# Two shifted patterns summed by accumulating transfers, and a further fill behind a run, in a one-core attention and MLP kernel

## The chip, the cores and the metric

The kernel runs on one core of a Trainium2 chip. The metric is the device time in microseconds of one execution. Three runs of the kernel before gave a median of 676.95 us (676.89 to 676.99).

## The reference

```python
def _A_ref(x, wq, wk, wv, wo):
    q = (x @ wq).reshape(B, S, H, Dh).transpose(0, 2, 1, 3)
    k = x @ wk
    v = x @ wv
    scores = jnp.einsum("bhqd,bkd->bhqk", q, k) * (Dh ** -0.5)
    p = softmax(scores, axis=-1)
    o = jnp.einsum("bhqk,bkd->bhqd", p, v)
    return o.transpose(0, 2, 1, 3).reshape(B, S, H * Dh) @ wo

def _B_ref(x, w1, w2):
    return silu(x @ w1) @ w2

xn = layernorm(x)
s = _A_ref(xn, wq, wk, wv, wo)
g = silu(_B_ref(xn, w1, w2))
return x + s * g
```

B = 1, S = 2048, D = 512, H = 32 heads of Dh = 16 that share one key and one value head, and an MLP width of F = 1792. Everything is bfloat16.

## The kernel before

The scores are worked out transposed: one block is 128 keys by 512 queries of one head. Queries come in four chunks of 512 and heads in eight groups of four, so there are 32 groups (chunk and four heads), each with 16 key tiles of four blocks: 2048 blocks. TensorE computes the four heads of a key tile in four row strips of its array (K is 16, padded to 32), and the products with the values in four column strips, in which a 17th column of ones gives the softmax's denominator. The results of a group accumulate in one PSUM bank, `psO`.

Two engines take the exponentials. ScalarE takes two blocks at a time out of `psA0` or `psA1` into one of eleven `pa_sb` buffers (`exp_A`, L576). VectorE takes one block at a time out of the banks `psD`, its second half `D1`, or `psF` (`exp_D`, L614): it adds a constant, clips at zero and rounds to int16, and these 16 bits read as bfloat16 are a rough exponential. The error is evened out by three such patterns of the same block, shifted by 0, 43 and 85 in the integer, with weights that are folded into three copies of the values (`vaug_sb`, filled by `evac_V`). GpSimd makes the two shifted patterns of a whole key tile with one 64-bit integer addition each (`shift`, L639). So a block of ScalarE's needs one product with the values (`emit_PV`, L698), and a block of VectorE's needs three. VectorE's patterns lie in four places (three in `ph_sb`, one in parts of `x_sb` once these are free), each with a buffer for each of the three patterns; `free_slot` picks a place and `may_D` says whether a place's old patterns have all been read.

The MLP and the projections are "jobs" (`emit_job`, L338): matmuls in column strips into `psF`, then a tanh on ScalarE (L1014) and a two-tensor operation on VectorE that makes a silu of it (L1046). A group's end is normalised by VectorE in four steps: `gn1` transposes `psO` (L769), `gn2` takes the reciprocal (L777), `gn3` multiplies (L786, two inputs in SBUF), `gn4` transposes back (L796). `final_add` (L1025) adds x, also with two inputs in SBUF, and stores the result from SyncE.

No engine orders itself: the class `Sched` keeps a model of each engine's time (`Sched.model`), and one Python loop at build time writes out all engines' instruction lists by it, with semaphore waits where one engine's work depends on another's. At each step the loop fills TensorE's column time in "slots" (four matmuls side by side) with jobs or products, and then issues a score run (`score_run`): the two blocks of ScalarE's next exponential, and, through `fill_D`, up to two blocks for VectorE into those banks that are free at that time. A new VectorE tile is taken from the end of its group's list of key tiles, ScalarE's from the beginning; a group's last three tiles are left to ScalarE (`LEAD = 3`) while VectorE begins the next group. `advance_v` settles the order on VectorE between evictions and the other tasks that `v_cand` offers. `held` tells whether a buffer has products left to be read; `filler` issues matmuls with zeros where TensorE would fall idle too long.

At the start ("front") x is loaded, the first four 128-row tiles are normalised (statistics by `stats`, L354, and `aggr`, L357, on VectorE, the root on ScalarE by `rstd_sqrt`, L368), and the rest follows beside the first groups.

Of the kernel before, what the change touches and what calls it, by code (L numbers as in the profile page):

```python
# [22 lines left out]
PH_SHIFT = (0, 43, 85)  # L23
PH_W = (0.2265625, 0.1787109375, 0.1416015625)
PH_ONE = 127 * 128
PH_BIAS = 65
NPH = len(PH_SHIFT)
LN2 = 0.6931471805599453
# [7 lines left out]
class Sched:  # L36
# [5 lines left out]
    def __init__(self):  # L42
        self.queues = {}
        self.done = {}
        self.clock = {}
        self.snap = {}
        self.last_w = {}
        self.readers = {}
        self.flagged = {}
        self.lanes = {}  # L50
        self.at = {}
        self.free = dict(pe=1.2, a=1.7, v=0.85, gp=0.7, sp=0.7)
        self.act_end = 0.0
        self.act_ends = []
        self.pe_mode, self.pe_last, self.pe_len, self.pe_tiles = None, 1.0, 0.0, set()
        self.pe_runs = []

# [37 lines left out]
    def model(self, eng, lane, cost, r):  # L95
        if lane:
            t = max(self.free[eng], r) + 0.05
            self.free[eng] = t
            return t + (cost or 3.0)
        if eng == "pe":  # L100
            mode, tiles, cols = cost or ("full", [None] * 4, 128)
            t = r
            for tile in tiles:
                if mode != self.pe_mode:
                    t = max(t, self.pe_last + self.pe_len + self.SWITCH)
                    self.pe_tiles = set()
# [17 lines left out]
        self.free[eng] = t + (cost or 0.4)  # L124
        return self.free[eng] + self.SEM
# [71 lines left out]
def bass_recurrent_scan__grouped_kv_mqa__dense_activation_silu__prompt_kernel(  # L197
# [39 lines left out]
    NPAIR, LEAD_PAIR = 1, 1  # L237
    NF, F_FROM, F_LEFT, F_LATE, DENSE_END, HOLD, F_BEHIND = 14, 0.05, 9, 3, 0.97, 10, 0

    with ExitStack() as es:  # L240
# [18 lines left out]
        ph_sb = [sb(f"ph{j}_sb", [P, NPS, 4 * NQ], I16) for j in range(NPH)]  # L259
# [13 lines left out]
        eps_sb = sb("eps_sb", [P, 1], FP32)  # L273
        mhalf_sb = sb("mhalf_sb", [P, 4], FP32)
# [80 lines left out]

        def aggr(t):
            op("v", lambda e: e.bn_aggr(mv_sb[:, t, :], stats_sb[:, t, :]), reads=[("st", t)], writes=[("mv", t)], cost=0.155)  # L357

        def rstd_pow(c):
            sl = slice(4 * c, 4 * c + 4)  # L360
            op("gp", lambda e: e.tensor_scalar(rstd_sb[:, sl], mv_sb[:, sl, 1], LN_EPS, None, op0=ALU.add),
               reads=[("mv", t) for t in tiles(c)], writes=[("rstd", c)])
            op("gp", lambda e: e.tensor_tensor(rstd_sb[:, sl], rstd_sb[:, sl], mhalf_sb[:, :], ALU.pow),  # L363
               reads=[("rstd", c), "mhalf"], writes=[("rstd", c)])
# [111 lines left out]
        for t in tiles(0):  # L476
            stats(t)
        for t in tiles(0):
            aggr(t)
# [121 lines left out]
        def ph_ap(j, sl, a, b):  # L601
            if sl < 3:
                return ph_sb[j][:, sl, a:b]
            return x_sb[:, 4 * j:4 * j + 4, :].rearrange("p a b -> p (a b)").bitcast(I16)[:, a:b]

        def ph_key(j, sl, p):
            return ("ph", j, sl, p) if sl < 3 else ("x", 4 * j + p)

        def exp_D(blks):
# [8 lines left out]
            for b in blks:  # L618
                p = b["pos"]
                owe(tile[0], b["i"], tile[1], 1, ph_ap(0, sl, 512 * p, 512 * p + 512).bitcast(BF16), ph_key(0, sl, p), K.at[d])  # L620
# [8 lines left out]
        shifts = []  # L629

        def shift(tile, idx):
            sl, n = slot_of[idx], len(rows_of[idx])
            for j in range(1, NPH):
                if n < 4:
                    d = op("v", lambda e, j=j: e.tensor_scalar(ph_ap(j, sl, 0, NQ * n), ph_ap(0, sl, 0, NQ * n), float(PH_SHIFT[j]), None,
                                                               op0=ALU.add),
                           reads=[ph_key(0, sl, p) for p in range(n)], writes=[ph_key(j, sl, p) for p in range(n)], cost=0.4)
                else:
                    d = op("gp", lambda e, j=j: e.int64_add(ph_ap(j, sl, 0, 4 * NQ).bitcast(I64), ph_ap(0, sl, 0, 4 * NQ).bitcast(I64),  # L639
                                                            PH_SHIFT[j] * 0x0001000100010001),  # L640
                           reads=[ph_key(0, sl, p) for p in range(4)], writes=[ph_key(j, sl, p) for p in range(4)], cost=1.03)
                for p, i in rows_of[idx].items():
                    owe(tile[0], i, tile[1], 1 + j, ph_ap(j, sl, 512 * p, 512 * p + 512).bitcast(BF16), ph_key(j, sl, p), K.at[d])

        def may_D(blks):
            sl = slot_of[blks[0]["idx"]]
            return not any(held(ph_key(j, sl, p)) for j in range(1, NPH) for p in range(4)) and \
                not any(held(ph_key(0, sl, b["pos"])) for b in blks)
# [8 lines left out]
        def emit_PV(t, cap):  # L657
# [7 lines left out]
            while n < cap:  # L665
                cand = sorted((p for p in pend[gi] if p["at"] <= t + 0.216 * n and vready(p["kt"] // 4, t)), key=lambda p: p["at"])
# [48 lines left out]
        def plan_D(gi, rows):  # L715
            owed[gi] += len(rows) * (NPH - 1)
            for i in rows:
                planned[gi][i] += NPH - 1
# [47 lines left out]
        def gn1(tk):  # L766
# [4 lines left out]
            task("gn2", gn2, 0.25, gi=gi, reads=[("otr", sl)], writes=[("rcp", sl)])  # L771
# [9 lines left out]
        def gn3(tk):  # L781
# [5 lines left out]
               reads=tk["reads"], writes=tk["writes"], cost=tk["cost"])  # L787
# [235 lines left out]
        def final_add(eng, tt, src, dst_key, queue="sp"):  # L1023
            slot = tt % NOB
            op(eng, lambda e: e.tensor_tensor(ob_sb[:, slot, :], src, x_sb[:, 12 + tt % 4, :], ALU.add),  # L1025
               reads=[dst_key, ("x", 12 + tt % 4)], writes=[("ob", slot)], cost=0.42)
# [52 lines left out]
        def free_slot(gi):  # L1079

            used = {slot_of[o["idx"]] for o in dst["open"] + dst["fifo"]}
            best = None
            for sl in range(NPD):
                if sl in used or (sl == 3 and not all(("nm", n) in tok for n in range(12))):
                    continue
                keys = {ph_key(j, sl, p) for j in range(NPH) for p in range(4)}
# [49 lines left out]
        def v_cand():  # L1136

            tv = K.free["v"] - 0.084
            cand = [(max(tv, K.ready("v", tk["reads"], tk["writes"])), tk) for tk in tasks if all(n in tok for n in tk["need"])]
            d, blks = 1e9, dst["fifo"][:1]  # L1140
            if blks and may_D(blks):
# [3 lines left out]
                if len(two) == 2 and (two[0]["bank"], two[1]["bank"]) == ("D", "D1") and two[0]["idx"] == two[1]["idx"] and may_D(two):  # L1145
                    d2 = max(tv, K.ready("v", ["D", "D1"], [ph_key(0, slot_of[b["idx"]], b["pos"]) for b in two]))
                    if d2 <= d + 0.1 and meets(d + 0.735) >= meets(d2 + 1.27):
# [29 lines left out]
        def target(t):  # L1177
# [9 lines left out]
            x = max(f, idle - 0.43)  # L1187
            return min(max(rel, x), need) if x <= need + SLIP else need

        def score_run(t):  # L1190
            t = max(t, release())
            if ast["tile"] is None and not left[group_A()]:
# [4 lines left out]
                if tanh_ready(K.act_end - 0.33):  # L1197
# [17 lines left out]
            if tanh_ready(K.act_end - 0.33):  # L1215
# [5 lines left out]
        def fill_D(t, free):  # L1221

            banks = sorted(free_banks(t + SLIP), key=lambda b: (b == "F", K.ready("pe", [], [b])))
            keep = 0
            if "F" in banks and jobs and behind(F_BEHIND) and next_job(t):
# [3 lines left out]
            for bank in banks[:max(0, len(banks) - keep)]:  # L1229
# [3 lines left out]
                if not pick and len(dst["open"]) < 2:  # L1233
# [30 lines left out]
        while state["g"] < NGRP or front or jobs or jst["open"] or tasks:  # L1264
            t = max(now, min(K.pe_next("col"), K.pe_next("full")))
            if t > 2000.0:
                raise ValueError(f"the order does not end {state} {jobs[:3]} {jst} {tasks} {dst} {ast}")
            advance_v(t + 0.05)
            more = group_A() < NGRP
            if tanh_ready(K.act_end - 0.33 if more else t):  # L1270
# [10 lines left out]
            if more:  # L1281
                last, aim = needed(), target(t)
                slots = min(4, int((last - t - K.SWITCH) / 0.2163), max(0, int((aim - t - K.SWITCH) / 0.2163 + ROUND)))
# [5 lines left out]
            if slots > 0:  # L1289
# [11 lines left out]
                if dense_first:  # L1301
# [9 lines left out]
                if can and not dense_first and slots > did:  # L1311
                    did += emit_job(t, slots - did)
            if more and not blocked:
# [3 lines left out]
                score_run(t)  # L1317
                now = 0.0
# [35 lines left out]
        def store(k, queue):  # L1354
            op(queue, lambda e: e.dma_start(ov[:, t0 + k, :], ob_sb[:, k, :]), reads=[("ob", k)], writes=[("out", t0 + k)], lane=f"st{k}{queue}")

# [64 lines left out]
```

## Time and profile before

| | before |
|---|---|
| median of the runs | 676.95 us (676.89 to 676.99) |
| profiled execution: time, span | 676.97 us, 675.0 us |
| busy TensorE, VectorE, ScalarE, GpSimd | 651.4, 588.9, 663.9, 369.1 us |
| exponentials on ScalarE (two blocks each) | 676 |
| evictions on VectorE (one block each) | 696 |
| shifts on GpSimd (INT64_ADD) | 348 |
| tanh on ScalarE | 72 |
| VectorE's waits for its score blocks in psD | 57.0 us |
| first exponential starts, last one ends | 10.49 us, 667.83 us |

The span runs from the first to the last instruction of the profiled execution; the rest of its time lies around it. "Busy" is the union of an engine's instructions. In the groups, a row has the line, engine and operation, what it writes and reads, the shapes and the count, then busy time and mean duration, then the engine's idle time before these instructions and what ended it. In the waits, a row has who waited for whom, the sum in us, the number of waits and the longest.

### The profile page before, as it was taken

What the parts mean: (1) busy time and instruction counts of PE and PEld (TensorE: products, weight loads), DVE (VectorE), ACT (ScalarE), POOL (GpSimd) and SP (SyncE); (2) the same over time, 40 slices, a digit from 0 to 9 for tenths busy, and PEclk for the clock granted to TensorE, in tenths of its full rate; (3) what the DMA queues carried; (4) which work ended last, traced back from release to release, by engine and by line L of the source; (5) the groups of instructions that cost most, each with busy time, mean ns of one, the idle gap of its engine ahead of it and who ended that gap; (6) DMA issues with size and microseconds to landing.
All of it is one profiled execution on the core that took longest, in us unless ns stands there. A gap on an engine that the chain in (4) does not pass through costs nothing.

```text
span 675.0 us, 18633 instructions
## 1 busy us (share of the span) xinstructions
PE 651.4 (96%) x8167; PEld 184.3 (27%) x8174; DVE 588.9 (87%) x1005; ACT 663.9 (98%) x762; POOL 369.1 (55%) x373
## 2 busy tenths in 40 slices
PE   8999999999999999999999999999999999999997
PEld 4422222222222222222222222222222222222221
DVE  7898788888798979999898988899898988888996
ACT  6999999999999999999999999999999999999997
POOL 3155455564555646565564655566564646654653
PEclk9999999999999999999999999999999999999999
DMA  6340000000000001000000000010000000000110
GB/s 178 134 146 2 1 2 1 2 2 1 2 1 2 2 17 34 18 1 2 2 1 2 1 2 2 1 33 18 17 2 2 2 2 1 2 2 1 34 33 32
DMA packets 12337, 12.50 MB, mean 19 GB/s; under 512 B 2528, under 2 KB 11744, under 8 KB 12256
## 3 DMA queue, kind: packets, MB, share of 16 engines
q1 hardware_dynamic: 11680, 10.78, 5.2%
q8 instruction: 64, 1.05, 0.7%
q10 hardware_dynamic: 576, 0.52, 0.2%
q14 instruction: 17, 0.14, 0.1%
HBM read 8.95 MB, written 2.10 MB: 16 GB/s over the span
## 4 chain that ended last, share of the span: by engine, by line
ACT 78%; PE 14%; DVE 3%; issue 1%; POOL 1%; DMA 1%; SPq 0%; POOLq 0%
ACT pa_sb L576 73%; PE psA L546 5%; ACT t_sb L1014 5%; PE psO L698 4%; PE psF L338 4%; DVE ph_sb L614 1%; DMA x_sb<-in_A_x_dram 1%; DVE stats_sb L354 1%; POOL ph_sb L639 1%; POOL rstd_sb L363 0%; DVE xn_sb L375 0%; PE psD L546 0%; PE psD L386 0%; PE psD L417 0%; DVE kTa_sb L429 0%
## 5 line engine op out<-in xcount | busy, mean ns | idle before, releaser
L576 ACT ACTIVATE pa_sb<-psA 128x1024 bf16<-128x1024 f32 x676 | 642.9, 1198 | 1.9 <-PE psA L546 1.7
L639 POOL INT64_ADD ph_sb<-ph_sb x290 | 300.7, 1049 | 221.8 <-DVE ph_sb L614 221.8
L614 DVE TENSOR_SCALAR ph_sb<-psD 128x512 int16<-128x512 f32 x527 | 351.8, 682 | 54.7 <-PE psD L546 47.9
L698 PE MATMUL psO<-ph_sb,vaug_sb 128*32 128x512 bf16 x1740 | 215.6, 383 | 0.2
L698 PE MATMUL psO<-pa_sb,vaug_sb 128*32 128x512 bf16 x1360 | 206.2, 383 | 0.4 <-ACT pa_sb L576 0.4
L546 PE MATMUL psA<-qT_sb,kTa_sb 32*128 32x512 bf16 x692 | 134.2, 385 | 6.8 <-ACT pa_sb L576 5.0
L546 PE MATMUL psA<-qT_sb,kTb_sb 32*128 32x512 bf16 x652 | 126.4, 384 | 7.9 <-ACT pa_sb L576 7.0
L546 PE MATMUL psD<-qT_sb,kTb_sb 32*128 32x512 bf16 x330 | 118.4, 384 | 0.4 <-DVE ph_sb L614 0.4
L546 PE MATMUL psD<-qT_sb,kTa_sb 32*128 32x512 bf16 x307 | 111.7, 384 | 0.1
L639 POOL INT64_ADD x_sb<-x_sb x58 | 60.2, 1050 | 49.7 <-DVE x_sb L614 49.7
L614 DVE TENSOR_SCALAR x_sb<-psD 128x512 int16<-128x512 f32 x110 | 74.2, 680 | 10.5 <-PE psD L546 9.1
L546 PEld LDWEIGHTS psA<-qT_sb,kTa_sb 32*128 32x128 bf16 x692 | 32.4, 91 | 148.2 <-ACT pa_sb L576 136.0
L338 PE MATMUL psF<-xnT_sb,w_sb 128*32 128x512 bf16 x896 | 70.4, 384 | 0.0
L546 PEld LDWEIGHTS psA<-qT_sb,kTb_sb 32*128 32x128 bf16 x652 | 30.6, 91 | 144.1 <-ACT pa_sb L576 136.6
L338 PE MATMUL psF<-w_sb,u_sb 128*32 128x512 bf16 x896 | 69.0, 384 | 0.0
L698 PEld LDWEIGHTS psO<-ph_sb,vaug_sb 128*32 128x32 bf16 x1740 | 53.4, 95 | 50.4 <-issue 33.8
L698 PEld LDWEIGHTS psO<-pa_sb,vaug_sb 128*32 128x32 bf16 x1360 | 50.6, 94 | 44.1 <-issue 33.2
L698 PE MATMUL psO<-x_sb,vaug_sb 128*32 128x512 bf16 x348 | 60.9, 384 | 0.0
L1014 ACT ACTIVATE t_sb<-psF 128x512 bf16<-128x512 f32 x72 | 56.6, 786 | 0.0
L1046 DVE SCALAR_TENSOR_TENSOR u_sb<-t_sb,psF 128x512 bf16<-128x512 bf16 x56 | 38.3, 683 | 6.1 <-ACT t_sb L1014 5.0
L614 DVE TENSOR_SCALAR ph_sb<-psF 128x512 int16<-128x512 f32 x53 | 35.9, 678 | 0.0
L546 PEld LDWEIGHTS psD<-qT_sb,kTb_sb 32*128 32x128 bf16 x330 | 28.2, 91 | 0.8 <-issue 0.7
(124 smaller groups left out, 351.6 us busy)
## 6 DMA issues: line engine op xcount, KB each, us to landing
w_sb<-in_B_w_dram SPq DMA_DIRECT2D x2, 1792.0 KB, 8.7
x_sb<-in_A_x_dram SPq DMA_DIRECT2D x18, 128.0 KB, 2.2
out_dram<-ob_sb SPq DMA_DIRECT2D x14, 128.0 KB, 1.7
x_sb<-in_A_x_dram SPq DMA_DIRECT2D x3, 512.0 KB, 7.1
wop_sb<-in_A_wo_dram SPq DMA_DIRECT2D x1, 512.0 KB, 5.6
wq_sb<-in_A_wq_dram SPq DMA_DIRECT2D x1, 384.0 KB, 6.7
x_sb<-in_A_x_dram ACTq DMA_DIRECT2D x2, 128.0 KB, 2.9
kTb_sb<-kTa_sb SPq DMA_DIRECT2D x16, 16.0 KB, 1.8
```

What stands on the lines that cost most here:

```text
L338: r = e.matmul(bank[32 * i:32 * i + 32, :], lhsT=lhsT[:, 32 * i:32 * i + 32], rhs=rhs, start=start, stop=stop, tile_position=(0, 32 * i), ...
L354: op("v", lambda e: e.bn_stats(stats_sb[:, t, :], x_sb[:, t, :]), reads=[("x", t)], writes=[("st", t)], cost=0.687)
L546: return e.matmul(ap, lhsT=kT_sb[g % 2][32 * i:32 * i + 32, kt * P:(kt + 1) * P], rhs=qT_sb[32 * i:32 * i + 32, c % 2, g // 2, :], start=T ...
L576: d = op("a", lambda e: e.activation(pa_sb[:, sl, :], psA[k][:, :], ACT.Exp, scale=ESCALE), reads=["A%d" % k], writes=[("pa", sl)], cost=2 ...
L614: d = op("v", lambda e: e.tensor_scalar(ph_ap(0, sl, 512 * pos, 512 * pos + m), src, float(PH_ONE + PH_BIAS), 0.0, op0=ALU.add, op1=ALU.ma ...
L639: d = op("gp", lambda e, j=j: e.int64_add(ph_ap(j, sl, 0, 4 * NQ).bitcast(I64), ph_ap(0, sl, 0, 4 * NQ).bitcast(I64), PH_SHIFT[j] * 0x0001 ...
L698: r = e.matmul(psO[32 * i:32 * i + 32, cs], lhsT=vaug_sb[:, p["v"], p["kt"], :], rhs=p["ap"], start=s0, stop=s1, tile_position=(0, 32 * i) ...
L1014: op("a", lambda e: e.activation(t_sb[:, n % 2, :], bank_ap(b), ACT.Tanh, scale=0.5 if jb[0] == "h" else 0.25), reads=[b], writes=[("t", n ...
L1046: op("v", lambda e: e.scalar_tensor_tensor(out=dst, in0=t_sb[:, n % 2, :], scalar=1.0, in1=src, op0=ALU.add, op1=ALU.mult), reads=tk["read ...
```

## The change

**Two patterns summed.** The shifts become 0, 42 and 88, and the first two patterns get the same weight (0.1953125). For a whole key tile that is started late enough before its group's end (at least `SUML` = 5 of the group's tiles left, or a tile of the next group; 9 in the last group; not in the front), GpSimd makes the pattern shifted by 42 and then issues a transfer within SBUF that adds the unshifted pattern to it in bfloat16. The sum needs one product with the values in place of two. The third pattern is then made in place over the unshifted one (`flush_later`), once the transfer has landed or, in a tile that isn't summed, once its products have been read. The model books 0.9 us of GpSimd for the issue and 4.7 us from issue to landing, and 2.8 us between two landings.

**Places of pairs.** A place now has two buffers instead of three, and there are six places instead of four (nine buffers in `ph_sb`, three in `x_sb`).

**Two-tensor operations put off.** The model now has VectorE's operations with two inputs in SBUF (`gn3`, `final_add`) wait for a GpSimd operation that is under way, and `v_cand` puts such a task off by up to 8 us (`PATIENCE`) while that wait would be over 0.2 us (`DEFER`), except in the last two groups.

**A further fill behind a run.** After a score run `extra_fill` gives one more block to a bank of VectorE's that is free or becomes free within 0.3 us (`XWAIT`), if by the model VectorE starts its next block more than 0.25 us (`XGAIN`) plus the waiting time sooner than with the next run's fill, and fewer than seven (`XHOLD`) of ScalarE's `pa_sb` buffers have products left.

**Smaller parts.** In the front, ScalarE makes the mean and the variance of the second tile by two activations with a sum (`stats_act`), and VectorE those of the other three. There are 13 warm-up matmuls instead of 15, and the jobs are spread from the 16th tile on instead of the 12th. ScalarE's two stores at the end become one. A fill by `row_want`, a longer run (`TWIN`) and other choices are in the code but switched off by the values in `RULES`, which hold for the whole run (`PLAN` is "A" alone); the limit `KEEP` for fillers goes from 0.65 to 0.6.

```diff
-PH_SHIFT = (0, 43, 85)
-PH_W = (0.2265625, 0.1787109375, 0.1416015625)
+PH_SHIFT = (0, 42, 88)
+PH_W = (0.1953125, 0.1953125, 0.1416015625)
...
+SUM_LAND = 4.7
...
     def model(self, eng, lane, cost, r):
+        if lane and eng == "gp":
+            t = max(self.free[eng], r + 0.25)
+            self.gp_runs.append((t, t + 0.9, True))
+            self.free[eng] = t + 0.92
+            self.sums = max(self.sums + 2.8, t + SUM_LAND)
+            return self.sums
...
-    NPD = 4
-    NPS = 3
+    SUML_END, DEFER, PATIENCE = 9, 0.2, 8
+    NPD = 6
+    NPB = 9
-    NWARM = 15
+    NWARM = 13
-    NFRONT = 12
+    NFRONT = 16
...
+        A=(0.2, 3.0, 0.6, 10, 1.2, 2.0, 0, 12, 0.2, 3, 3, 0.0, 0.25, 0.43, 0, 0.33, 0, 0, 5, 9, 0.3, 7),
...
-        ph_sb = [sb(f"ph{j}_sb", [P, NPS, 4 * NQ], I16) for j in range(NPH)]
+        ph_sb = sb("ph_sb", [P, NPB, 4 * NQ], I16)
...
+        def stats_act(t):
+            r = D ** -0.5
+            op("a", lambda e: e.activation(scr_sb[:, 1:2], eps_sb[:, 0:1], ACT.Sqrt), ...)
+            op("a", lambda e: e.activation(t_sb[:, 0, :], x_sb[:, t, :], ACT.Copy, scale=1.0 / D, accum_out=mv_sb[:, t, 0:1]), ...)
+            op("a", lambda e: e.activation(nm_sb[:, 0:1], mv_sb[:, t, 0:1], ACT.Copy, scale=r), ...)
+            op("a", lambda e: e.activation(t_sb[:, 1, :], x_sb[:, t, :], ACT.Square, scale=-r, bias=nm_sb[:, 0:1],
+                                           accum_out=mv_sb[:, t, 1:2]), ...)
...
         def shift(tile, idx):
...
+            flush_later(K.ready("gp", first, other_))
+            d = op("gp", lambda e: e.int64_add(whole(1, sl), whole(0, sl), PH_SHIFT[1] * 0x0001000100010001),
+                   reads=first, writes=other_, cost=1.03)
+            if idx in summed:
+                d = op("gp", lambda e: e.dma_start(whole(1, sl, dt=BF16), whole(0, sl, dt=BF16), accum_op=ALU.add),
+                       reads=first, writes=other_, lane=f"sum{sl}")
+            owe_D(tile, idx, 1, 2, K.at[d])
...
+            later.append(dict(tile=tile, idx=idx, sl=sl, at=K.at[d] if idx in summed else None))
...
+        def flush_later(t):
+            for x in list(later):
...
+                if x["at"] > t + 0.1 if x["at"] is not None else any(held(k) for k in first):
+                    continue
+                later.remove(x)
...
+                    d = op("gp", lambda e, sl=sl: e.int64_add(whole(0, sl), whole(0, sl), PH_SHIFT[2] * 0x0001000100010001),
+                           reads=first, writes=first, cost=1.03)
+                owe_D(x["tile"], x["idx"], 0, 3, K.at[d])
...
+                    if DEFER < 9 and tk["kind"] in ("gn3", "add") and state["g"] < NGRP - 2:
+                        end = K.lock(x + 0.13)
+                        if end > x + DEFER and x < tk.setdefault("due", x + PATIENCE):
+                            x = end - 0.13
...
+        def extra_fill():
+            t = K.pe_last + K.pe_len
+            if sum(held(("pa", k)) for k in range(NPA)) >= XHOLD or group_A() >= NGRP or ...:
+                return
+            advance_v(t + 0.05)
+            vfree = K.free["v"] + 0.62 * len(dst["fifo"]) + ...
+            ride = max(needed(), t + 0.2) + 0.43
...
+                    r = max(t, K.ready("pe", [], [b]))
+                    gain = max(vfree, ride) - max(vfree, r + 0.43)
+                    if r <= t + XWAIT and gain > XGAIN + XCOST * (r - t):
...
+            fill_D(best[0], [0, 1, 2, 3], [best[1]])
...
-                        plan_D(new[0], rows)
                         dst["idx"] += 1
+                        if not front and len(rows) == 4 and (new[0] > group_A() or len(left[new[0]]) >= (SUML_END if new[0] == NGRP - 1 else SUML)):
+                            summed.add(dst["idx"])
+                        plan_D(new[0], rows, NPH - (dst["idx"] in summed))
...
         warm(NWARM, psF[:, :], "F")
-        for t in tiles(0):
+        stats_act(1)
+        for t in (0, 2, 3):
             stats(t)
...
-        store(0, "a")
         copy(1, ob_sb[:, 1, :], ("ob", 1), bank_ap("D1"), "D1")
-        store(1, "a")
+        op("a", lambda e: e.dma_start(ov[:, t0:t0 + 2, :], ob_sb[:, 0:2, :]), ...)
```

More of the change, by code (lines that the diff above doesn't have):

```diff
@@ L56, in __init__ @@
         self.pe_runs = []
+        self.gp_runs, self.tt_runs = [], []
+        self.sums = 0.0
+        self.next_gp = 1e9
     def deps(self, eng, reads, writes):
@@ L627, in exp_D, with whole, spare @@
                     shifts.append((tile, idx))
-        shifts = []
+        shifts, summed, later = [], set(), []
+        def whole(j, sl, n=4, dt=I64):
+            return ph_ap(j, sl, 0, n * NQ).bitcast(dt)
+        def spare(sl):
+            busy = {slot_of[o["idx"]] for o in dst["open"] + dst["fifo"]} | {x["sl"] for x in later} | {slot_of[a[1]] for a in shifts} | {sl}
+            for m in range(NPD):
+                if m not in busy and not any(held(ph_key(j, m, p)) for j in range(2) for p in range(4)):
+                    if 2 * m + 1 < NPB or all(("nm", n) in tok for n in range(12)):
+                        return m
+            return None
@@ new lines, in shift @@
+            if sl2 is not None:
+                d = op("gp", lambda e: e.int64_add(whole(0, sl2), whole(0, sl), PH_SHIFT[2] * 0x0001000100010001),
+                       reads=first, writes=[ph_key(0, sl2, p) for p in range(4)], cost=1.03)
+                owe_D(tile, idx, 0, 3, K.at[d], sl2)
+                return
+            later.append(dict(tile=tile, idx=idx, sl=sl, at=K.at[d] if idx in summed else None))
+            K.next_gp = min([x["at"] for x in later if x["at"] is not None], default=1e9)
```

202 lines of the change are left out of this document (157 added, 45 removed).

## The prediction

> **What bounds the kernel now.** I read the page first. ScalarE is busy for nearly the whole span, TensorE and VectorE a little less, and the clock is full in every slice.
>
> ```profile
> PE 651.4 (96%) x8167; PEld 184.3 (27%) x8174; DVE 588.9 (87%) x1005; ACT 663.9 (98%) x762; POOL 369.1 (55%) x373
> ```
>
> The chain of waits shows what ScalarE's time is made of.
>
> ```profile
> 226.34 3.67 ACT pa_sb L576 x4
> 230.00 0.49 ACT t_sb L1014
> 230.50 11.00 ACT pa_sb L576 x12
> ```
>
> Exponentials of two score blocks follow each other every 11.00/12 = 0.917 us, and a tanh adds 0.49 us. 675 x 0.917 + 72 x 0.49 = 654 us; with the first exponential's start (10.5), its own 1.2, 7.2 after the last and about 2 of stalls, that is the span of 675.0. The profiled execution took 676.97 (1.97 outside the span) and the median of the runs is 676.95, so I work from the median. Nothing but fewer exponentials, a shorter front or a shorter tail can shorten this kernel. The groups show who takes the other blocks.
>
> ```profile
> L576 ACT ACTIVATE pa_sb<-psA 128x1024 bf16<-128x1024 f32 x676 | 642.9, 1198 | 1.9 <-PE psA L546 1.7
> L639 POOL INT64_ADD ph_sb<-ph_sb x290 | 300.7, 1049 | 221.8 <-DVE ph_sb L614 221.8
> L614 DVE TENSOR_SCALAR ph_sb<-psD 128x512 int16<-128x512 f32 x527 | 351.8, 682 | 54.7 <-PE psD L546 47.9
> L698 PE MATMUL psO<-ph_sb,vaug_sb 128*32 128x512 bf16 x1740 | 215.6, 383 | 0.2
> L786 DVE TENSOR_TENSOR onb_sb<-otr_sb,rcp_sb 128x256 bf16<-128x256 f32 x31 | 16.1, 520 | 0.0
> ```
>
> VectorE evicts 527 + 110 + 53 + 6 = 696 blocks, 174 key tiles of four, and GpSimd makes two shifted patterns of each (290 + 58 = 348). All 2048 blocks are 2 x 676 + 696. So a tile given to VectorE instead of ScalarE takes two exponentials, 1.834 us, off the span. What stops VectorE from taking more is in the waits and the timeline.
>
> ```profile
> DVE ph_sb L614 <- PE psD L546: 47.9, 168, 1.6
> DVE x_sb L614 <- PE psD L546: 9.1, 35, 0.7
> DVE u_sb L1046 <- ACT t_sb L1014: 5.0, 18, 1.0
> ```
> ```profile
> 306.07 0.39 PE L546 MATMUL psA<-qT_sb,kTa_sb 32*128 32x512 bf16 x2
> 306.08 0.38 PE L546 MATMUL psD<-qT_sb,kTa_sb 32*128 32x512 bf16 x1
> ...
> 306.54 0.69 DVE L614 TENSOR_SCALAR ph_sb<-psD 128x512 int16<-128x512 f32 x1 [0.39 <-PE psD L546]
> 306.62 0.39 PE L338 MATMUL psF<-xnT_sb,w_sb 128*32 128x512 bf16 x4
> 306.94 0.39 PE L546 MATMUL psA<-qT_sb,kTa_sb 32*128 32x512 bf16 x2
> ...
> 307.41 0.69 DVE L614 TENSOR_SCALAR ph_sb<-psD 128x512 int16<-128x512 f32 x1 [0.18 <-PE psD L546]
> ```
>
> A bank for VectorE is filled only inside a score run (306.08, 306.95). When the run comes, the other bank is still being read, so one run fills one bank, VectorE works 0.69 us of it and waits for the next. These waits (with psF, 2.2 + 0.7 more) sum to 59.9 us. TensorE has little room to be kinder: run to first column matmul 0.33, one slot 0.22, last slot to run 0.32, so a run costs 0.43 beyond its slots, and two slots make 0.87 of the 0.917.
>
> **The sums.** A tile started while at least five of its group's key tiles are left, or for the next group, needs two products with the values instead of three: four matmuls, one slot, fewer. Of 174 I count as unsummed about 13 (the one step between five left and the lead of three, in 32 groups of some 5.5 tiles), 4 to 6 of the front and a few of the last group: 155 are summed. That is 155 x 0.22 = 34 us of TensorE's 676 x 0.43 + 1474 x 0.22 = 615. By itself it gains nothing on ScalarE's chain, since TensorE held ScalarE up for 1.9 us only.
>
> **The further fill.** After a run a bank that frees within 0.3 us is filled if VectorE starts 0.25 us sooner for it. In the timeline's pattern the bank being read frees about 0.25 us after the run's start, so the rule bites where the single waits stand, and chains of them vanish. A fill costs TensorE 0.22 to 0.5 us, I take 0.3; 100 of them cost 30 us, which the sums have paid. I take 40 of the 59.9 us as filled; the bounds are 15 (only a long wait meets the rule) and 54 (nine tenths).
>
> **GpSimd and two-tensor operations.** GpSimd gets 155 issues more. No row shows one; the nearest are SyncE's issue of 512 KB (0.51) and the INT64_ADD (1.05), and I take 1.0 as both act on the same buffers: 181 x 2 x 1.05 + 155 = 535 us, 81% of a shorter span. That matters to VectorE. The group of L786 has a mean of 520 ns and a shortest of 406: some of its operations take 600 to 1207 ns, and each of these starts inside an INT64_ADD and ends 0.27 us after it. Over 31 of these and the 12 at L1025 the loss is 3.9 us now. Put off while GpSimd is busy, for up to 8 us, I let it double (4 us more); where putting off fails, a mean wait of 0.65 us in 43 operations is 28, or 24 more. The Trainium skill ("SBUF — State Buffer", Who interferes with whom) says that a VectorE instruction with two SBUF inputs and a GpSimd one that reads SBUF exclude each other for a whole instruction; the stretched rows agree.
>
> **The balance.** A tile moved to VectorE gives it four evictions, 4 x 0.60 back to back (in the timeline two of 0.68 take 1.30 together at 304.85), and shortens its span by 1.834: 4.23 us of its idle time. (40 - 4)/4.23 = 8.5 tiles, 15.6 us. TensorE then has 659 runs x 0.43, 1290 slots x 0.22 and 100 fills x 0.3: 597 us in about 642, against 615 in 657 before: it still fits.
>
> **Front, tail, planner.** One tile's statistics go to ScalarE, which waits 2.9 us there; VectorE's chain of four statistics (2.52) and aggregates (0.36) loses about 0.7, but ScalarE's three small operations on a tile that lands a little later fill much of it, and ScalarE's later stalls of 0.1 to 0.7 us up to 34 us eat an earlier start: 0 to 0.6, I take 0.3. Two stores become one that ends before the last ones of SyncE, which cover it (without them, some 0.6); two warm-up matmuls fewer lie in TensorE's idle start: nothing. A fixed order with transfers in it runs less closely to its plan: ScalarE's stalls, 2 us now, grow by 0 to 8, I take 2. **Sum: 676.95 - 15.6 - 0.3 + 2 = 663.1.**
>
> A tile now holds a pair of buffers through its fill (3.7), a shift (1.05), the landing, the second shift and some 3 us until its products, 13.5 in all; with a tile every 3.6 us that is 3.8 of six places, so places do not stop it.
>
> **The transfer.** Where the sum can fall is its landing. The code books 4.7 us. The rows: 16 KB within SBUF land in 1.8, 1792 KB in 8.7, so 512 KB between them in 1.8 + 496 x 6.9/1776 = 3.7; if the destination's reading counts as well, 5.7; the slowest 512 KB row, among other loads, has 7.1.
>
> ```profile
> w_sb<-in_B_w_dram SPq DMA_DIRECT2D x2, 1792.0 KB, 8.7
> x_sb<-in_A_x_dram SPq DMA_DIRECT2D x3, 512.0 KB, 7.1
> kTb_sb<-kTa_sb SPq DMA_DIRECT2D x16, 16.0 KB, 1.8
> ```
>
> I take the middle of the first two, 4.7, as the DMA engines are all but idle after 40 us. One transfer starts every 660/155 = 4.3 us and by the same slope moves for 1.9 to 3.9, so the queue holds. Behind a late one GpSimd waits with the next shift, then TensorE with its product and all runs after it.
>
> **Rivals.**
> (A) The forecast: 40 to 54 us filled with stalls small, or 30 filled with stalls of 5: 655 to 669. Chance 0.60.
> (B) TensorE takes the gain back: further fills cost it slots, the products pile up, and the rule's limit of seven held tiles of ScalarE switches the fills off. 15 filled, 4 lost: 2.6 tiles, 4.8 us, so 673.9; down to nothing, 677. For it: two slots already make 0.87 of 0.917. Against it: 34 us of slots are freed. Chance 0.15, 0.03 of it within 0.2%.
> (C) GpSimd at 81% holds VectorE: the 24 us above leave 40 - 24 = 16, 3.8 tiles, 6.9 us: 671.8. For it: the stretched rows at 55%. The rule of the Trainium skill's page "SBUF — State Buffer" is this case, taken without the putting off. Chance 0.10.
> (D) The other side: sums land late. TensorE's order has some 1.1 us of cover (a run of ScalarE's buffer, 0.92, and 4.3 x 0.05 of slack). A tile issued while another is under way shifts with it, so about every second late landing counts: 78 x (landing - 4.7 - 1.1). It decides from a landing of 6.0, where it eats the 14 us; at 6.5 the time is 663 + 55 = 718. For it: the 7.1 row. Against it: idle DMA engines. Chance 0.13.
> (E) GpSimd needs other code for issuing transfers. Its first INT64_ADD waited 5.8 us and the last change back 6.7 (waits of L512 and L1273, on "issue"); 12.5 x 155 would make some 1900 us. No row excludes it; the issue's cost would show at once. Chance 0.02.
>
> **How the numbers follow.** The likeliest is (A), 663. A measurement tells 0.2% (1.4 us) from no change. Faster: 0.60 + 0.12 + 0.10 = 0.82; same 0.03; slower 0.13 + 0.02 = 0.15. Range: (D) and (E) lie outside, 0.15. The low end is 54 us filled and nothing lost to two-tensor operations or stalls: 54/4.23 = 12.8 tiles, 23.4 us, and 0.6 of the front give 653, and I write 652. Above it reaches to 676, with (C) and nearly all of (B).
>
> **What would show it.** Right: 650 to 665 exponentials, about 155 transfers issued by GpSimd that land in 4 to 6 us, L614's waits for psD near 20 us, VectorE busy above 90%, ScalarE idle below 8. (B): these waits above 40 us and over 670 exponentials. (C): L786's mean above 900 ns. (D): few exponentials, but ScalarE waits for psA, TensorE for GpSimd or the transfer, tens of us. Wrong altogether: as many exponentials as before.

## The result, and the profile after

The changed kernel takes 702.39 us in the median of four runs (696.58 to 707.74), where 663 was forecast. Over the fast runs alone, three of the four, it takes 1.0346 times the time before (interval 1.0316 to 1.0377), which is 23.4 us more, and the differences between kernels below are taken from such ratios. The profiled execution took 698.72 us with a span of 696.9, 21.9 us above the span before, and the readings below are of that execution.

The engines' line and the clock's line of the page of the changed kernel:

```profile
PE 657.7 (94%) x7515; PEld 187.0 (27%) x7517; DVE 606.4 (87%) x993; ACT 661.7 (95%) x758; POOL 518.1 (74%) x538
...
PEclk9999989979999999999999999999999999999998
```

ScalarE now has idle time, where before it had next to none. The groups (columns as in the table's note above):

```profile
L640 ACT ACTIVATE pa_sb<-psA 128x1024 bf16<-128x1024 f32 x666 | 633.0, 1116 | 24.6 <-PE psD L610 13.8
L687 DVE TENSOR_SCALAR ph_sb<-psD 128x512 int16<-128x512 f32 (+1 forms) x587 | 397.4, 706 | 53.2 <-PE psD L610 48.1
L762 POOL INT64_ADD ph_sb<-ph_sb x155 | 186.5, 1227 | 59.0 <-DMA ph_sb<-ph_sb 45.5
```

Ten exponentials are fewer (666 for 676), as 2048 = 2 x 666 + 716 blocks on VectorE. Their cadence is still 0.917 us and a tanh still adds 0.49. What the time from the first exponential's start to the last one's holds beyond this cadence is called ScalarE's stalls from here on: 29.9 us, and 1.9 before. The sum of the span: first exponential at 10.2, 665 x 0.917, 72 x 0.49, 29.9 of stalls, the last exponential's own 1.0, and 10.7 after it, the tail: 697. Before, the tail was 7.2. So 9.2 us were saved in exponentials and 0.3 in the front, and 28.0 came back as stalls and 3.5 as tail.

Some of the waits of the changed kernel (who waited for whom, us, times, longest):

```profile
DVE ph_sb L687 <- PE psD L610: 48.1, 133, 1.9
POOL ph_sb L762 <- DMA ph_sb<-ph_sb: 45.5, 38, 6.5
ACT pa_sb L640 <- PE psD L610: 13.8, 23, 2.9
POOL ph_sb L762 <- DMA x_sb<-ph_sb: 12.7, 12, 3.4
DVE x_sb L687 <- PE psD L610: 12.1, 37, 2.5
PEld psO L819 <- DMA ph_sb<-ph_sb: 10.1, 11, 3.1
ACT pa_sb L640 <- PE psA L610: 9.8, 11, 4.3
```

VectorE waits as long for its score blocks as before: 48.1 + 12.1 = 60.2 us against 57.0. New are the waits on transfers: GpSimd for landings before it may make the third pattern, and TensorE for sums that it is to multiply. What ScalarE sees of both is a score run that comes late (the ends of its waits are the run's matmuls, L610).

**First sums.** The timeline (start, duration, engine and line, and in brackets the idle time before and what ended it) of GpSimd, and below it of ScalarE:

```profile
35.93 1.17 POOL L737 DMA_DIRECT2D ph_sb<-ph_sb  x1 [0.32 <-POOL ph_sb L734]
...
38.81 0.88 POOL L737 DMA_DIRECT2D ph_sb<-ph_sb  x1 [0.31 <-POOL ph_sb L734]
46.20 1.03 POOL L762 INT64_ADD ph_sb<-ph_sb  x1 [6.51 <-DMA ph_sb<-ph_sb]
```
```profile
39.48 4.77 ACT L640 ACTIVATE pa_sb<-psA 128x1024 bf16<-128x1024 f32 x5
47.12 1.02 ACT L640 ACTIVATE pa_sb<-psA 128x1024 bf16<-128x1024 f32 x1 [2.87 <-PE psD L610]
```

The sum issued at 35.93 is waited for until 46.1: 10.2 us, among the loads of the MLP's and the output's weights. GpSimd stands still for 6.51 us, TensorE for 2.77 and ScalarE for 2.87.

**One two-tensor operation.** GpSimd, then VectorE, 100 us later:

```profile
140.40 0.87 POOL L737 DMA_DIRECT2D ph_sb<-ph_sb  x1 [0.30 <-POOL ph_sb L734]
141.01 1.36 POOL L762 INT64_ADD ph_sb<-ph_sb  x1
142.02 1.35 POOL L734 INT64_ADD ph_sb<-ph_sb  x1
143.03 2.35 POOL L762 INT64_ADD ph_sb<-ph_sb  x2
```
```profile
140.91 4.76 DVE L908 TENSOR_TENSOR onb_sb<-otr_sb,rcp_sb 128x256 bf16<-128x256 f32 x1
145.60 0.68 DVE L687 TENSOR_SCALAR ph_sb<-psD 128x512 int16<-128x512 f32 x1
```

The multiplication `gn3`, 0.41 us by itself, starts inside an issue and ends 0.29 us after the last of the four INT64_ADDs queued behind that issue (145.38). VectorE evicts nothing for 4.6 us, so neither of its banks comes free, TensorE's fixed order stands before a fill, and ScalarE's next blocks are behind that fill: it stands still for 4.27 us until 148.06, the longest of the waits on psA above. TensorE's own row:

```profile
146.33 0.60 PE L610 MATMUL psD<-qT_sb,kTa_sb 32*128 32x512 bf16 x1 [3.82 <-DVE ph_sb L687]
```

This matmul takes 0.60 us where such a one took 0.38 at 141.27: TensorE's granted clock is at half here. The last section shows such stretches; much of ScalarE's stalls lies in them.

**The fills.** By the order and times of the score matmuls, some 690 of 696 blocks for VectorE were filled inside a run before and some 6 behind one; after, of 716, some 615 inside and some 100 behind. The further fills came, but they took the place of over 70 fills inside the runs: some ten more runs than before fill no bank at all.

### The profile page after: what moved, and what is told of

It reads as the page before. It is cut to its first block, busy times and chain, and to the rows that moved or that the text cites. A ratio compares the mean times of both kernels' runs of the same rounds, so it can differ in the third digit from the quotient of the medians.

```text
span 696.9 us, 17463 instructions
## 1 busy us (share of the span) xinstructions
PE 657.7 (94%) x7515; PEld 187.0 (27%) x7517; DVE 606.4 (87%) x993; ACT 661.7 (95%) x758; POOL 518.1 (74%) x538
## 4 chain that ended last, share of the span: by engine, by line
ACT 26%; PE 25%; DMA 21%; POOL 15%; DVE 8%; issue 4%; POOLq 0%; SPq 0%
ACT pa_sb L640 24%; DMA ph_sb<-ph_sb 13%; PE psA L610 9%; PE psO L819 7%; PE psF L389 6%; POOL ph_sb L734 5%; DMA x_sb<-ph_sb 5%; POOL ph_sb L762 5%; DVE ph_sb L687 4%; POOL x_sb L734 2%; DMA x_sb<-x_sb 2%; PE psD L610 2%; ACT t_sb L1136 2%; POOL ph_sb L737 2%; DVE onb_sb L908 1%
## 5 line engine op out<-in xcount | busy, mean ns | idle before, releaser
L687 DVE TENSOR_SCALAR ph_sb<-psD 128x512 int16<-128x512 f32 (+1 forms) x587 | 397.4, 706 | 53.2 <-PE psD L610 48.1
L762 POOL INT64_ADD ph_sb<-ph_sb x155 | 186.5, 1227 | 59.0 <-DMA ph_sb<-ph_sb 45.5
L819 PE MATMUL psO<-pa_sb,vaug_sb 128*32 128x512 bf16 x1340 | 168.0, 387 | 4.1 <-DMA ph_sb<-ph_sb 2.4
L734 POOL INT64_ADD ph_sb<-ph_sb x131 | 154.6, 1183 | 15.9 <-DVE ph_sb L687 15.4
L819 PE MATMUL psO<-ph_sb,vaug_sb 128*32 128x512 bf16 x1248 | 149.0, 390 | 8.0 <-DMA ph_sb<-ph_sb 4.4
L610 PE MATMUL psA<-qT_sb,kTa_sb 32*128 32x512 bf16 x688 | 134.1, 387 | 4.4 <-ACT pa_sb L640 3.7
L610 PE MATMUL psD<-qT_sb,kTb_sb 32*128 32x512 bf16 x369 | 130.8, 385 | 2.4 <-DVE ph_sb L687 1.9
L610 PE MATMUL psA<-qT_sb,kTb_sb 32*128 32x512 bf16 x636 | 124.6, 391 | 3.0 <-ACT pa_sb L640 2.3
L737 POOL DMA_DIRECT2D ph_sb<-ph_sb x109 | 95.7, 878 | 33.7 <-POOL ph_sb L734 33.7
L610 PE MATMUL psD<-qT_sb,kTa_sb 32*128 32x512 bf16 x331 | 113.0, 393 | 5.4 <-DVE ph_sb L687 4.6
L687 DVE TENSOR_SCALAR x_sb<-psD 128x512 int16<-128x512 f32 (+1 forms) x83 | 57.5, 704 | 12.3 <-PE psD L610 12.1
L610 PEld LDWEIGHTS psA<-qT_sb,kTa_sb 32*128 32x128 bf16 x688 | 32.3, 91 | 130.8 <-ACT pa_sb L640 106.5
L610 PEld LDWEIGHTS psA<-qT_sb,kTb_sb 32*128 32x128 bf16 x636 | 29.8, 91 | 124.6 <-ACT pa_sb L640 96.7
L819 PEld LDWEIGHTS psO<-ph_sb,vaug_sb 128*32 128x32 bf16 x1248 | 37.0, 95 | 49.0 <-issue 24.7
L819 PE MATMUL psO<-x_sb,vaug_sb 128*32 128x512 bf16 x280 | 40.3, 387 | 1.8 <-POOL x_sb L762 1.0
L734 POOL INT64_ADD x_sb<-ph_sb x26 | 30.7, 1182 | 8.9 <-DVE ph_sb L687 8.7
## 6 DMA issues: line engine op xcount, KB each, us to landing
w_sb<-in_B_w_dram SPq DMA_DIRECT2D x2, 1792.0 KB, 11.9
```

Source lines behind the costliest of these rows:

```text
L610: return e.matmul(ap, lhsT=kT_sb[g % 2][32 * i:32 * i + 32, kt * P:(kt + 1) * P], rhs=qT_sb[32 * i:32 * i + 32, c % 2, g // 2, :], start=T ...
L687: d = op("v", lambda e: e.tensor_scalar(ph_ap(0, sl, 512 * pos, 512 * pos + m), src, float(PH_ONE + PH_BIAS), 0.0, op0=ALU.add, op1=ALU.ma ...
L734: d = op("gp", lambda e: e.int64_add(whole(1, sl), whole(0, sl), PH_SHIFT[1] * 0x0001000100010001), reads=first, writes=other_, cost=1.03)
L737: d = op("gp", lambda e: e.dma_start(whole(1, sl, dt=BF16), whole(0, sl, dt=BF16), accum_op=ALU.add), reads=first, writes=other_, lane=f"s ...
L762: d = op("gp", lambda e, sl=sl: e.int64_add(whole(0, sl), whole(0, sl), PH_SHIFT[2] * 0x0001000100010001), reads=first, writes=first, cost ...
L819: r = e.matmul(psO[32 * i:32 * i + 32, cs], lhsT=vaug_sb[:, p["v"], p["kt"], :], rhs=p["ap"], start=s0, stop=s1, tile_position=(0, 32 * i) ...
```

## The experiments

Two suspects stand for the 28 us of stalls: sums that land late (the prediction's D), and two-input operations caught by GpSimd (its C). A third was that the further fill upsets the order whatever the sums do. Five kernels keep the instruction order of the change: two take away one cause each, one takes both away, one adds waits, and one only copies.

**f_oneinput.** `gn3` and all but the last additions of x become fills with a constant; normalisation and most of the output are left out.

```diff
-e.tensor_tensor(d3, o3, rcp_sb[...], ALU.mult)
+e.memset(d3, 0.0625)
-e.tensor_tensor(ob_sb[:, slot, :], src, x_sb[...], ALU.add)
+e.memset(ob_sb[:, slot, :], 0.5)       # for tt < NT - 4
```

> The changed kernel's instruction order, with VectorE's two-input operations (the multiply of gn3, the addition of final_add but for the last four) replaced by fills with a constant, which read nothing; the normalisation and the residual are left out. If VectorE's two-input operations that wait behind GpSimd's chains (up to 4.8 us each in the changed kernel's trace) make the stalls, some 16 of ScalarE's 30 us of stalls go and the time is about 684 to 690. If late landings make them, it stays near 700.

Measured: 689.18 us, ratio 1.0173 (1.0139 to 1.0206), stalls of 20.4 us. That is 11.7 us less than the change: caught two-input operations are a cause, and not the only one. ScalarE's wait near 148 us is gone, and the one for the first sum is still there:

```profile
47.44 1.02 ACT L640 ACTIVATE pa_sb<-psA 128x1024 bf16<-128x1024 f32 x1 [3.00 <-PE psD L610]
```

**f_quarter.** Only one of a tile's four blocks is summed, so a transfer has 128 KB for 512; three quarters of the summed pattern stay unsummed. The count and cost of issues stay.

```diff
-e.dma_start(whole(1, sl, dt=BF16), whole(0, sl, dt=BF16), accum_op=ALU.add)
+e.dma_start(whole(1, sl, n=1, dt=BF16), whole(0, sl, n=1, dt=BF16), accum_op=ALU.add)
```

> The changed kernel's order, with each accumulating transfer cut to a quarter (128 KB, one of four blocks), so that three quarters of the sums are left out. If late landings (4.5 to 10.2 us against the booked 4.7) make the stalls, landings fall to about 3 us and the time to 685 or below. If the two-input operations make them, it falls by the 4 us of the first two landings only, to about 696.

Measured: 687.1 us, ratio 1.0151 (1.0128 to 1.0173), stalls of 20.6; the time is 2 us above what was expected. The issues of the two, columns line, count, KB each and median us to landing, first of the change, then of this kernel:

```profile
ph_sb<-ph_sb POOLq DMA_DIRECT2D x109, 512.0 KB, 5.0
```
```profile
ph_sb<-ph_sb POOLq DMA_DIRECT2D x109, 128.0 KB, 2.7
```

With landings of 2.7 us instead of 5.0, 13.2 us are gone. Late sums are the second cause. Here the wait near 47 us is gone, and the one for a held `gn3` remains:

```profile
141.41 1.02 ACT L640 ACTIVATE pa_sb<-psA 128x1024 bf16<-128x1024 f32 x1 [4.04 <-PE psA L610]
```

**f_both.** Both edits at once.

> Both of these at once (normalisation, residual and three quarters of the sums left out). If landings and two-input operations are all there is, the run follows its plan: 666 exponentials with 2 to 5 us of stalls, 666 to 672 us. If it stays above 680, a third cause is there: TensorE waiting in its fixed order for VectorE's banks, or its clock.

Measured: 669.2 us, ratio 0.9883 (0.9868 to 0.9897): faster than the kernel before, with stalls of 0.9 us. One group and some waits of this kernel:

```profile
L640 ACT ACTIVATE pa_sb<-psA 128x1024 bf16<-128x1024 f32 x666 | 632.8, 1198 | 1.3 <-PE psD L610 0.6
```
```profile
DVE ph_sb L687 <- PE psD L610: 42.0, 128, 1.4
...
DVE x_sb L687 <- PE psD L610: 8.9, 35, 0.7
...
POOL ph_sb L762 <- DMA ph_sb<-ph_sb: 5.4, 3, 3.7
```

The two causes together are worth 31.3 us, 6.4 more than 11.7 + 13.2 (3 to 10 more, by an estimate from the four intervals), and without them nothing of size stalls ScalarE in this order. The tail stays at 10.1 us. The same order with the same fills still leaves VectorE 50.9 us of waits for score blocks.

**f_gate.** Can a wait keep GpSimd out of the way? `gn3` and `final_add` write a key that GpSimd's instructions read, so that an instruction built after such an operation waits for it. The order is the change's.

```diff
-reads=first, writes=other_, cost=1.03)
+reads=first + ["port"], writes=other_, cost=1.03)
-reads=tk["reads"], writes=tk["writes"], cost=(0.41,))
+reads=tk["reads"], writes=tk["writes"] + ["port"], cost=(0.41,))
```

> The changed kernel with nothing left out and the same order, but GpSimd's shifts and issues wait for a two-input operation that stands before them in the build order, so that it waits for one GpSimd instruction and not for a chain. If the chains behind an issue are what holds VectorE, this gives some 10 us: 690 to 694. If late landings make the stalls, no change: 698 to 706.

Measured: 698.92 us (694.01 to 706.26), ratio 1.0361 (1.0296 to 1.0427), not told apart from the change; its trace has stalls of 25.4 us. VectorE's timeline of this kernel still has

```profile
224.71 3.06 DVE L912 TENSOR_TENSOR onb_sb<-otr_sb,rcp_sb 128x256 bf16<-128x256 f32 x1
```

The two INT64_ADDs that hold it start at 225.11 and 226.12, before it is done, so they don't wait for it: they were built ahead of it, and no such wait covers them. The excess of all 43 operations over 0.41 us fell only from 15.8 to 13.4 us.

**f_plain.** What of a landing is the adding? The transfer only copies, and the sum becomes a copy of the unshifted pattern.

```diff
-e.dma_start(whole(1, sl, dt=BF16), whole(0, sl, dt=BF16), accum_op=ALU.add)
+e.dma_start(whole(1, sl, dt=BF16), whole(0, sl, dt=BF16))
```

> The changed kernel's order with the transfers as plain copies within SBUF of the same 512 KB: the sums are left out (the pattern is overwritten). If reading the destination makes the landing, it falls from a median of 5.0 us to 3.5 to 4.0 and the time by some 10 us; if the issue and the queue make it, it stays near 5.

Measured in one execution: 688.26 us, stalls of 20.8, as with the quarter. The issues on GpSimd (ns: shortest, median, longest), of the change and then of this kernel:

```profile
L737 POOL DMA_DIRECT2D ph_sb<-ph_sb x109: 867/874/1172, 35.9 to 676.7; - x109
```
```profile
L737 POOL DMA_DIRECT2D ph_sb<-ph_sb x109: 545/547/859, 36.2 to 668.0; - x109
```

The landing of the same transfers, from the issues of this kernel's page:

```profile
ph_sb<-ph_sb POOLq DMA_DIRECT2D x109, 512.0 KB, 2.9
```

So adding costs 0.33 us of an issue and 2.1 us of a landing, and the DMA engines' share from 100 to 660 us doubles (0.34 to 0.69). The Trainium skill ("DMA: Bandwidth & Descriptors", Anatomy of one DMA, the gpsimd path) fits 2.0 us plus the bytes at 436 GB/s to a transfer that GpSimd issues, by which an estimate for 512 KB is 3.2 us. That is near the copy's 2.9 in this trace, and 1.8 below the accumulating 5.0.

Then come kernels in which the program orders its work anew, the first two with one part of the change switched off.

**p_nosum.** No tile is summed; places of pairs and the further fill stay.

```diff
-if not front and len(rows) == 4 and (new[0] > group_A() or ...):
+if False and (new[0] > group_A() or ...):
```

> The whole change without the sums: every VectorE tile keeps three products, GpSimd issues no transfer, the further fill stays. The order is planned anew and has 682 exponentials, 6 more than before. If the stalls come from transfers and from two-input operations behind an issue, this one runs close to its plan: 682 x 0.917 + 72 x 0.49 + about 21 = 681 to 685, slower than before through its exponentials alone. If the further fill itself upsets TensorE's order, stalls over 10 us show and it is above 690.

Measured: 681.17 us, ratio 1.0062 (1.0045 to 1.0079); 682 exponentials, stalls of 1.0, some 50 fills behind a run.

**e_nofill.** The sums stay, the further fill is switched off (`XGAIN` 0.25 to 9).

> The change without the further fill (its gain threshold set out of reach); 147 tiles are summed. The planned order has 680 exponentials. By the forecast's steps the sums alone gain nothing: 676 to 680. By late landings and two-input operations behind issues it has stalls like the changed kernel's: 695 to 710. If it has few stalls, the further fill is what upsets the order.

Measured: 702.33 us, ratio 1.0363 (1.0335 to 1.0392); 680 exponentials, stalls of 22.2. Under these rules neither half cuts exponentials (682, 680); with both there are 666. The fills do need the slots that the sums free, as the prediction had it. But 22.2 us of stalls remain without any further fill, and p_nosum has 1.0: the stalls come with the sums.

**v_tol.** An order meant to bear both causes: sums only after 52 us and with eight tiles left, 3.4 us between landings, `gn3` booked at 0.7 us, and other values in `RULES`.

```diff
-self.sums = max(self.sums + 2.8, t + SUM_LAND)
+self.sums = max(self.sums + 3.4, t + SUM_LAND)
-A=(..., 0.25, 0.43, 0, 0.33, 0, 0, 5, 9, 0.3, 7),
+A=(..., 0.35, 0.43, 0, 0.28, 0, 0, 8, 9, 0.3, 7),
```

> A tolerant order with sums and further fill: a tile is summed only if at least eight of its group's key tiles are left and after 52 us (119 summed tiles instead of 155, none beside the loads of the second MLP weight), landings are booked 3.4 us apart, and the normalisation's multiply is booked at 0.7 us. It plans 672 exponentials. If late landings and the two-input operations are the cause, most stalls go: 672 to 682, near the kernel before. If the cause lies elsewhere: above 690.

Measured: 681.15 us, ratio 1.0062 (1.0047 to 1.0077); 672 exponentials, stalls of 5.3, and GpSimd still waits 52.2 us for landings of `ph_sb`.

**v_late1, v_late2, v_late3.** GpSimd's work is put in its list only when the model has it nearly free (`GPAHEAD`), so that a two-input operation can be placed ahead of it, and the waits of f_gate are there and visible to the model. Landings are booked at 5.6 us (the first two) or 5.2, and summing starts at 58 or 46 us. The three differ in how many tiles they sum: 133, 117, 102. Each, like v_tol, is the best by the kernel's own model of many orders with different values in `RULES`.

```diff
-SUM_LAND = 4.7
+SUM_LAND = 5.6
+def lazy(t):
+    while shifts and ... and K.free["gp"] <= t + GPAHEAD:
+        shift(*shifts.pop(0))
```

> An order that tolerates what the runs showed: GpSimd gets an instruction only when it is within 1.8 us of being free and waits for a two-input operation that stands before it; landings are booked at 5.6 us and 3.4 us apart; sums start after 58 us, and a tile is summed if at least six of its group's key tiles are left (133 sums). 672 exponentials are planned. If late landings and chains behind an issue are the whole cause, stalls stay below 4 us and the time is 672 to 677, at or a little below the kernel before. If other losses come with the transfers, it is above 680.

> The same with fewer sums (117: at least eight key tiles left, from 46 us on, a further fill only for a gain over 0.45 us) and GpSimd within 2.5 us of being free; 672 exponentials. If the two causes are all there is: 672 to 677; otherwise above 680.

> The same with still fewer sums (102: at least ten key tiles left), landings booked at 5.2 us, GpSimd within 1.5 us of being free; 672 exponentials. If the two causes are all there is: 672 to 677, the least stalls of the three; otherwise above 680.

Measured: 674.77, 674.81 and 674.97 us, ratios 0.9962 (0.9949 to 0.9975), 0.9968 (0.9955 to 0.9981) and 0.9975 (0.9965 to 0.9985). All have 672 exponentials and stalls of 1.1, 2.1 and 0.4 us. An order that leaves room does carry over a hundred sums without stalls, and is 2 us faster than the kernel before.

**v_none.** The control: the same search, the same late placing, places of pairs and further fill, with no sums at all.

> A control for the three tolerant orders, searched in the same way and over as many orders: no tile is summed, the rest of the change stays, with a further fill for a gain over 0.6 us. 673 exponentials, one more than theirs. If their 674.8 comes from the choice of a good order and not from the sums, this one is as fast: 674 to 676. If the sums carry it, this one lies at 677 or above.

Measured: 672.62 us (672.47 to 672.75), ratio 0.9936 (0.9922 to 0.9950). This is the fastest kernel that computes everything, 4.3 us better than before, and it sums nothing. A group of it:

```profile
L643 ACT ACTIVATE pa_sb<-psA 128x1024 bf16<-128x1024 f32 x673 | 639.3, 1198 | 0.6 <-PE psA L613 0.6
```

Its span is 4.3 us shorter. Three exponentials fewer than before (2.8 us), no stalls beyond the cadence instead of 1.9 (2.1, as it runs 0.2 ahead of 0.917 each), and a first exponential at 10.15 instead of 10.49 make 5.2, and its tail is 0.9 us longer. With some 20 fills behind runs it comes within one exponential of the orders that sum. So what the v_late kernels gained came from the choice of the order or from the change's other parts, which v_none shares, and in these orders sums added nothing on top of it. Which of the two it was, no run tells apart.

## Why the prediction was wrong, point by point

- **Counts and single costs held.** 155 transfers were forecast and issued. An issue was taken at 1.0 us: 0.87 and 0.30 of idle time ahead of it, with part of it overlapped by the INT64_ADD behind. The landing was taken at 4.7 between 3.7 and 5.7; the median is 5.0. The front gained the 0.3. GpSimd was busy for 518 us (535 forecast). (E) is excluded: no issue waited for other code.
- **"I take 40 of the 59.9 us as filled"** failed, below its bound of 15. The step reasoned from one run's pattern at 306 us and took each further fill as an addition. In the ordered program most took the place of a fill inside the next run: about 100 came, as forecast, and the waits for psD were 60.2 us, against 57.0 before. Even in f_both 50.9 remain. VectorE gained 5 tiles, not 8.5; the seven exponentials of difference are 6.4 us. f_both, without the stalls, stands 6.0 us above the forecast: these 6.4 and a tail that is 2.9 longer, against 3 us that the forecast had as stalls and f_both lacks.
- **"ScalarE's stalls grow by 0 to 8, I take 2"** failed most, and is the step that turned the sign: they grew by 28.0. f_both shows what they were, 31.3 us with both causes, of the 37.3 by which the forecast was too low; the other 6.0 is the point above. The prediction put the tail at no change; it grew by 3.5, and by 2.9 in f_both too, so the two causes don't explain it, and its cause stays open.
- **The balance's 1290 slots** don't follow from 1474 less 155, which is 1319 and more with the moved tiles. The difference is some 8 us of TensorE that would still have fitted, so nothing hangs on it.
- **(D)** named the mechanism and its path (GpSimd, then TensorE's product, then all runs behind it), and priced it from a threshold on the typical landing: "It decides from a landing of 6.0". The median of 5.0 was below it, and it decided all the same: 27 of the 155 landings took longer than the 5.8 us (4.7 booked, 1.1 of cover) that it allowed. Landings spread from 4.5 to 10.2 us, with a median of 5.8 where the preceding issue was under 2.5 us before and 4.6 where it was 4.5 or more. The first two, 10.2, were beside loads: the row of 7.1 "among other loads" was the warning, and "the DMA engines are all but idle after 40 us" was asked of the wrong stretch, since sums start at 36 us.
- **(C)** priced VectorE's lost time (24 us spread over 43 operations, as fewer tiles). The measured excess is 15.8 us, 11.9 more than before and within its bound. The price is another: a few long holds, up to 4.76 us, stop the banks and with them TensorE's fixed order and ScalarE's chain. Without two-input operations 11.7 us come back. Putting off did not prevent this; f_gate suggests why, since the instructions that hold a `gn3` were built ahead of it and run later than the model has them.
- (C) and (D) were separate cases with 0.10 and 0.13. They came together. That late landings lengthen the holds of `gn3` does not show: in f_quarter, with landings of 2.7 us, the excess of the 43 operations is 19.4 us, more than the change's 15.8. The traces point to the clock for what f_both has beyond the sum: either cause alone still brings stretches at half clock, and only without both are there none (the last section). This is read off, not isolated.
- **(B)'s** idea that further fills take back what the sums give was not it: f_both and p_nosum against each other (666 and 682 exponentials, 669.2 and 681.2 us) suggest that under the change's own rules the sums pay for the fills, if they land in time and hold nobody; f_both leaves out the normalisation, so its time is no measure of a whole kernel.

What stays open: moving the late loads away from the first sums in an otherwise unchanged order was not tried, and the spread of the landings by their distance is a reading of one trace.

## What to carry to other kernels

An order fixed at build time turns the spread of a new operation into a stall of every engine behind it: price the slowest landings and the longest hold against the slack of the order, not the median against a threshold. A freed resource is worth only what the bounding engine can do with it; read how many units move, since an added action can displace one that was there already. And before a searched order's gain is put down to a new part, search as hard without that part: here the control was the fastest of all that compute everything.

## What the runs showed of the hardware

- A two-input VectorE operation that starts inside one INT64_ADD ended 0.27 us after it, in the kernel before, and in six of ten cases there it did so although a second INT64_ADD followed at once. In the changed kernel one that starts inside GpSimd's issue of a transfer waits for the INT64_ADDs queued behind it without a gap as well: four of them, 4.76 us in all, and two in f_gate, 3.06 us. The Trainium skill ("SBUF — State Buffer", Who interferes with whom) gives the lock for one whole instruction; here several in a row went first.
- An INT64_ADD behind an issue shows 1.36 us instead of 1.04: it begins some 0.26 us before the issue's record ends, and the next one follows 1.01 us later.
- TensorE's granted clock fell to half in four stretches of the changed kernel before its end, 23.8 us in all, where the kernel before has none. Each begins within 3 us of the end of an idle time of TensorE, 2.77, 0.84, 3.82 and 1.03 us long. Two of them (stretch, length, busy time of TensorE, its weight loads, VectorE, ScalarE and GpSimd, clock, DMA share, GB/s); the others are 97.7 to 104.5 and 268.4 to 271.8:

```profile
46.50:49.90 3.40, 3.40 (x29) 0.61 (x25) 0.96 (x2) 2.05 (x2) 3.10 (x4) 0.50 0.71 196
145.50:155.70 10.20, 9.37 (x62) 1.99 (x66) 7.12 (x12) 5.20 (x6) 4.60 (x5) 0.50 0.27 51
```

Of ScalarE's 29.9 us of stalls 16.2 fall to exponentials that start in these stretches or up to 1.5 us behind them, 8.7 of it without the two waits of 2.87 and 4.27 us. By the same count it is 9.1 of 20.4 us in f_oneinput, 14.5 of 20.6 in f_quarter and nothing in f_both, whose clock is 1.00 from 34 to 660 us. So the stalls bring the half clock with them, and further stalls lie in it; that the slower matmuls make these was not isolated. The clock is not the whole: e_nofill has 4.9 of 22.2 us there. An idle time of 1.26 us that ends at 319.7 brought no such stretch, so what decides is not shown.
